# The last head group of a linear-attention numerator: six matmuls over 72 rows against four over 108

## The chip, the cores and the metric

The kernel runs on one core of one Trainium2 chip. Its metric is the device time in microseconds (us) from one launch. Times of several runs are given by their median.

TensorE (PE) multiplies matrices; its weight loads (PEld) and its matmuls are separate instructions that overlap. VectorE (DVE), ScalarE (ACT) and GpSimd (POOL) do elementwise work. SyncE (SP) issues most transfers (DMAs). ACT and POOL also issue some. Each engine takes its instructions strictly in the order of its own queue.

## The reference

The whole layer is a gated linear-attention block with a feed-forward branch, in float32, with 2048 tokens, width 576, 32 heads of 18, and a hidden width of 4608:

```
xn  = layernorm(x)
q, k, v = xn @ wqkv, split into 32 heads of 18
pq, pk  = q @ w_phi, k @ w_phi            (per head, 18 x 18)
phi_q   = concat(softmax(pq), softmax(-pq))    # 36 features per head
phi_k   = concat(softmax(pk), softmax(-pk))
kv  = phi_k^T v        (per head, 36 x 18);   z = sum over tokens of phi_k
num = phi_q kv;        den = phi_q z + 1e-6
s   = (num / den) @ wo
g   = silu( (silu(xn @ w_gate) * (xn @ w_up)) @ w_down )
out = x + s * g
```

The change concerns `num`, which the code computes in a function called `numer`.

## The kernel before

**Precision.** Matmuls run on operands of a shortened float32 type (`F32R`). To keep accuracy every operand is held as a high part and a low part: `split(hi, lo, src)` casts `src` into `hi` on ACT and subtracts on DVE to get `lo`. A product then takes three matmuls, high by high, low by high and high by low.

**Stages.** Tokens are normalised and transposed (0 to about 80 us), then for each of 16 token tiles of 128 the key features and the values are computed and `kv` is summed in three PSUM banks `kvp` (`k_tile`, `kv_step`, up to about 217 us). Then comes the setup for the queries (lines 530 to 565): the bank's column of `z` is spread into `zb`, each bank is masked so that only the 18 x 18 blocks of one head stay (`km`, line 558), and split into `KVH` and `KVL` (line 560, helper lines 62 and 63). From about 220 to 455 us runs the query stage; after about 476 us the feed-forward products run to the end.

**Head groups.** Seven heads make a group of 126 columns. There are `NG` = 5 groups: four of 126 and a last one of `NL` = 72 columns (4 heads). For each group and each of the two softmax signs (`s`), `KVH[:, 2 * g + s]` is a block-diagonal matrix of kv.

**The query stage.** `q_tile` makes the unnormalised features of 128 tokens, `e` of 128 x 1152 (first 576 columns for one sign, then 576 for the other), scales them by the softmax sums and the denominator (line 626, the last write of `e`) and returns them. `numer` takes two such tiles (`QS` = 256 tokens). For each group it transposes the group's columns of both tiles and both signs with PE into `pt` (line 638, four transposes), splits them into `ph` and `pl` (line 641), and adds up six matmuls into `po` (line 645): `KVH` by `ph`, `KVL` by `ph`, `KVH` by `pl`, each for two signs. The result is split into `oh` and `ol`. The last group goes first. Its result takes another form: the high part is written into `om` (tile name `km`) twice, and 36 rows of the low part are put under each by a transfer (`km<-lo`, line 653), so that `om` has `NK` = 108 rows and the projection with `wo` needs two matmuls for this group and not three. `project` multiplies by `wo` (line 672) and stores. There are 8 calls of `numer`.

**Order of work.** The program's order is a wish: a planner places each instruction on its engine's queue by costs that it assumes, and the marks `tc.high_priority()` and `tc.issue_after(...)` move single ones. So PE mixes three things in the query stage: the query products (line 96, `p<-QH,X` and `p<-QL,X`), the numerators and projections, and early strips of the feed-forward products (`early_tile`, line 96, `pe<-X,wh` and `pe<-X,wl`), which depend on neither. Their weights come through `raw` (line 113) and the casts of lines 66 to 68.

**SP's queue at the seam.** In order: stores of `sum_dram` (lines 366, 367), loads of `wo` (577), loads of `tl` (592), a store of `h_dram` (136), then the `raw` loads (113).

**Buffers.** Pools marked `reuse_waits="tile"` hand memory on when the old tile's readers are done. `phi` is the name of the key features' two buffers, which nothing uses after the last `kv_step`.

Of the kernel before, what the change touches and what calls it, by code (L numbers as in the profile page):

```python
# [9 lines left out]
F32 = mybir.dt.float32  # L10
F32R = mybir.dt.float32r
# [6 lines left out]
S, D, H, DH, F = 2048, 576, 32, 18, 4608  # L18
P = 128
# [7 lines left out]
GW = GH * DH  # L27
GROUPS = [(g * GW, min(GW, D - g * GW)) for g in range((D + GW - 1) // GW)]
NG = len(GROUPS)
NL = GROUPS[-1][1]  # L30
NK = NL + NL // 2
QS = 256
EARLY = 4
FIRST = (EARLY + 1, EARLY)
# [7 lines left out]
def heads(ap):  # L42
    return ap.rearrange("p (h d) -> p h d", d=DH)


def spread(ap, n):
    return ap.unsqueeze(2).to_broadcast([P, n, DH])
# [3 lines left out]
def gated_hedgehog_kernel(ctx: ExitStack, tc, x, w_qk, w_v, w_phi, wo, w_gu, w_tail, w_down, ident_in, mask_in, out):  # L51
# [5 lines left out]
    nc = tc.nc  # L57
# [3 lines left out]
    def split(hi, lo, src):  # L61
        nc.scalar.copy(hi, src)  # L62
        nc.vector.tensor_sub(lo, src, hi)  # L63
# [19 lines left out]
    def block(t):  # L83
        return t // HT, (t % HT) // 4, slice((t % 4) * P, (t % 4 + 1) * P)
# [55 lines left out]
    with ExitStack() as att:  # L140
        const = att.enter_context(tc.tile_pool(name="const", bufs=1))
        ident = const.tile([P, P], F32, name="ident")
# [15 lines left out]
        with ExitStack() as wst:  # L158
# [144 lines left out]
            kk = kst.enter_context(tc.tile_pool(name="kk", bufs=2, side="right", reuse_waits="tile"))  # L303
# [134 lines left out]
            def k_tile(t):  # L438
                i0, j0, cols = block(t)
                pk = kps.tile([P, 2, 512], F32, name="p2")  # L440
                for i in range(2):
                    w = slice(i * HALF, (i + 1) * HALF)
                    xw(pk[:, i, 0:HALF], i0, j0, cols, KVWH[:, :, :, w], KVWL[:, :, :, w], True)
                phi = kk.tile([P, 2 * D], F32, name="phi", bufs=2)
                sm = softmax_parts(pk, phi)
                nc.vector.reciprocal(sm, sm)
                nc.vector.tensor_mul(heads(phi), heads(phi), spread(sm, 2 * H))
                return phi
# [18 lines left out]
            for p in range(8):  # L467
                k = (p + 4) % 8
                ts = [k // 4 * HT + k % 4 + 4 * j for j in range(2)]
                if p < 2:  # L470
                    for j, t in enumerate(ts):
                        phi = k_tile(t)
# [56 lines left out]

        with ExitStack():  # L530
            qc = att.enter_context(tc.tile_pool(name="qc", bufs=1, reuse_waits="tile"))
            KVH = qc.tile([GW, 2 * NG, GW], F32R, name="KVH")
            KVL = qc.tile([GW, 2 * NG, GW], F32R, name="KVL")
            zb = qc.tile([P, 2 * D], F32, name="zb")
            zc = qc.tile([GW, 12], F32, name="zc")
            m4 = mask.rearrange("p h d -> p (h d)")
            banks = [(i, 4 if i < 2 else 2, GROUPS[2 * i][1]) for i in range(3)]
            for i, n, w in banks:
                nc.scalar.copy(zc[0:w, 4 * i:4 * i + n], kvp[i][0:w, 0:n, w])
            z2, oz = zb.rearrange("p (s n) -> p s n", s=2), GROUPS[-1][0]  # L540

            def z_rows(d, g, s):
                w = GROUPS[g][1]
                nc.tensor.matmul(d, zc[0:w, 2 * g + s:2 * g + s + 1].to_broadcast([w, P]), ident[0:w, 0:w],
                                 start=True, stop=True)

            for s, name in enumerate(("vx", "vy")):
                zp = kps.tile([P, 512], F32, name=name)
                for g, (o, w) in enumerate(GROUPS[:-1]):
                    z_rows(zp[:, o:o + w], g, s)  # L550
                nc.scalar.copy(z2[:, s, 0:oz], zp[:, 0:oz])
            zp = kps.tile([P, 512], F32, name="vx")
            for s in range(2):
                z_rows(zp[:, s * NL:(s + 1) * NL], NG - 1, s)
            nc.scalar.copy(z2[:, :, oz:D], zp[:, 0:2 * NL].rearrange("p (s n) -> p s n", s=2))
            for i, n, w in banks:
                km = qc.tile([GW, 4, GW], F32, name="km")
                nc.vector.tensor_mul(km[0:w, 0:n, 0:w], kvp[i][0:w, 0:n, 0:w],
                                     m4[0:w, 0:w].unsqueeze(1).to_broadcast([w, n, w]))
                split(KVH[0:w, 4 * i:4 * i + n, 0:w], KVL[0:w, 4 * i:4 * i + n, 0:w], km[0:w, 0:n, 0:w])  # L560

        raw_x(order[7], 0, 1)
        raw_x(order[7], 2, 3)
# [4 lines left out]
        with ExitStack() as qst:  # L568
            qw = qst.enter_context(tc.tile_pool(name="qw", bufs=1, reuse_waits="tile"))
            qk = qst.enter_context(tc.tile_pool(name="qk", bufs=2, reuse_waits="tile"))  # L570
# [8 lines left out]
            def split_wo():  # L579
# [4 lines left out]
                for a, t in enumerate((WOH, WOL)):  # L584
                    nc.sync.dma_start(t[NL:NK, NG - 1].bitcast(F32), WOH[a * (NK - NL):a * (NK - NL) + NK - NL, NG - 1].bitcast(F32))

# [20 lines left out]
            def q_tile(t):  # L607
                i0, j0, cols = block(t)
                pq = qps.tile([P, 2, 512], F32, name="p2")
                for i in range(2):  # L610
                    w = slice(i * HALF, (i + 1) * HALF)
                    xw(pq[:, i, 0:HALF], i0, j0, cols, QH[:, :, :, w], QL[:, :, :, w], True)
                e = qk.tile([P, 2 * D], F32, name="e", bufs=4)
                r = softmax_parts(pq, e).rearrange("p (s h) -> p s h", s=2)
                ez = qk.tile([P, 2 * D], F32, name="ez", bufs=1)
                nc.vector.tensor_mul(ez, e, zb)
                y = qk.tile([P, 2 * H], F32, name="y")
                nc.vector.reduce_sum(y, heads(ez), axis=AX.X)
                y2 = y.rearrange("p (s h) -> p s h", s=2)
                nc.vector.scalar_tensor_tensor(y2[:, 0], r[:, 0], DEN_EPS, y2[:, 0], op0=ALU.mult, op1=ALU.add)  # L620
                nc.vector.tensor_mul(y2, y2, r[:, ::-1])
                den = qk.tile([P, H], F32, name="den")
                nc.vector.tensor_add(den, y2[:, 0], y2[:, 1])
                nc.vector.reciprocal(den, den)
                nc.vector.tensor_mul(y2, r[:, ::-1], den.unsqueeze(1).to_broadcast([P, 2, H]))
                last_e.append(nc.vector.tensor_mul(heads(e), heads(e), spread(y, 2 * H)))
                return e

            def numer(es):
                oh = qk.tile([GW, NG - 1, QS], F32R, name="oh", bufs=1)  # L630
                ol = qk.tile([GW, NG - 1, QS], F32R, name="ol", bufs=1)
                om = qc.tile([NK, 2, QS], F32R, name="km")
                for g in (NG - 1, *range(NG - 1)):
                    o, w = GROUPS[g]
                    pt = qps.tile([GW, 2, QS], F32, name="pt", bufs=2)
                    for s in range(2):
                        for j, e in enumerate(es):
                            nc.tensor.transpose(pt[0:w, s, j * P:(j + 1) * P], e[:, s * D + o:s * D + o + w], ident)
                    ph = qk.tile([GW, 2, QS], F32R, name="ph", bufs=2)
                    pl = qk.tile([GW, 2, QS], F32R, name="pl", bufs=2)  # L640
                    split(ph[0:w], pl[0:w], pt[0:w])
                    po = pt[:, 0]
                    for k, (a, p) in enumerate(((KVH, ph), (KVL, ph), (KVH, pl))):
                        for s in range(2):
                            nc.tensor.matmul(po[0:w], a[0:w, 2 * g + s, 0:w], p[0:w, s], start=k + s == 0, stop=k + s == 3)
                    if g < NG - 1:
                        split(oh[0:w, g], ol[0:w, g], po[0:w])
                        continue
                    lo = qk.tile([NL, QS], F32R, name="lo", bufs=1)
                    nc.scalar.copy(om[0:NL], po[0:NL].unsqueeze(1).to_broadcast([NL, 2, QS]))  # L650
                    nc.vector.tensor_sub(lo, po[0:NL], om[0:NL, 0])
                    for a in range(2):
                        nc.sync.dma_start(om[NL:NK, a].bitcast(F32), lo[a * (NK - NL):a * (NK - NL) + NK - NL].bitcast(F32))
                return oh, ol, om

            def project(b, oh, ol, om, last):
                for j in range(QS // P):
# [3 lines left out]
                    for i in range(2):  # L661
# [7 lines left out]
                        mm = [(a[:, g, jc], bw[:, g, n]) for g in range(NG - 1) for a, bw in ((oh, WOH), (oh, WOL), (ol, WOH))]  # L669
                        mm += [(om[:, a, jc], bw[0:NK, NG - 1, n]) for a, bw in enumerate((WOH, WOL))]  # L670
                        for k, (a, bw) in enumerate(mm):
# [495 lines left out]
    for i, n, f in units:  # L1167
# [3 lines left out]
        if f >= FIRST[i]:  # L1171
            w = kept.pop() if i and kept else ready.pop(0)
# [6 lines left out]
        if n % 2 == 0:  # L1179
            g = {"f": (f, units[units.index((i, n, f)) + 1][2]), "h": [h]}  # L1180
# [58 lines left out]
```

## Time and profile before

| what | value |
|---|---|
| median of 3 runs | 1592.99 us (1592.48 to 1593.02) |
| profiled execution, its own time | 1592.74 us |
| its span, first to last instruction | 1590.6 us |
| granted TensorE clock, mean | 0.999 |
| matmuls | 9383 |
| PE, PEld busy | 1578.2 us (99%), 1416.1 us (89%) |
| DVE, ACT, POOL busy | 1166.5 (73%), 724.8 (46%), 662.3 us (42%) |

An instruction's row has its start, its duration, its engine, its line, the tiles that it writes and reads, its shape, and in square brackets the time that the engine stood idle before it with what ended the wait. "x2" is two instructions merged into one row from the first start to the last end. A busy PE is modelled: matmuls overlap in a pipeline, so the distance between two starts is what a matmul takes of PE's time, and not its duration.

### The profile page before, as it was taken

To read this page: it belongs to the slowest core of one execution; us is meant where nothing else is said; L and a number is where in the kernel's file an instruction comes from. 1 tells how busy PE (TensorE), PEld (TensorE's weight loads), DVE (VectorE), ACT (ScalarE), POOL (GpSimd) and SP (SyncE) were. 2 spreads that over 40 slices of the span, in tenths; PEclk is the share of its full clock that TensorE was granted. 3 is DMA by queue.
4 is the path that set the end of the run, shared out by engine and by line. 5 is a ranking of instruction groups with operands and counts; after the bars stand their busy time and mean duration, and the time that the engine had idled before them with its cause. 6 is when DMAs were issued, how large, how long until landed. Compare 5 with 4: busy or idle time off the path is not lost.

```text
span 1590.6 us, 25333 instructions
## 1 busy us (share of the span) xinstructions
PE 1578.2 (99%) x9383; PEld 1416.1 (89%) x9383; DVE 1166.5 (73%) x1729; ACT 724.8 (46%) x1403; POOL 662.3 (42%) x714
## 2 busy tenths in 40 slices
PE   9999999999999999999999999999999999999998
PEld 6899998999988988988888898888888888888887
DVE  7777769999946778887777778645767667666677
ACT  5633345455435654454544554454443343333334
POOL 3676762433116535554545445223324324133133
PEclk9999999999999999999999999999999999999999
DMA  9622244445447554555455453974545655555445
GB/s 306 200 82 81 95 145 129 119 122 163 165 175 245 174 178 174 176 177 180 174 174 200 163 186 116 337 219 151 154 139 156 192 177 160 176 184 184 142 118 179
DMA packets 124044, 269.03 MB, mean 169 GB/s; under 512 B 13194, under 2 KB 54858, under 8 KB 122642
## 3 DMA queue, kind: packets, MB, share of 16 engines
q1 hardware_dynamic: 108476, 245.49, 47.2%
q0 software_dynamic: 3552, 12.59, 2.7%
q10 hardware_dynamic: 11894, 9.35, 1.8%
q8 instruction: 74, 1.21, 0.3%
q14 instruction: 48, 0.39, 0.1%
HBM read 167.53 MB, written 99.09 MB: 168 GB/s over the span
## 4 chain that ended last, share of the span: by engine, by line
PE 67%; DVE 1%; POOL 1%; DMA 0%; issue 0%; ACT 0%; SPq 0%; POOLq 0%
PE px L790 25%; PE pd L911 24%; PE pw L790 12%; PE py L790 6%; DMA hb<-h_dram 0%; POOL acc L949 0%; PE pe L96 0%; DVE w L63 0%; DVE hh L63 0%; DMA out<-acc 0%; ACT w L62 0%; POOL ld L769 0%; DVE X L940 0%; POOL ha L1050 0%; DVE X L1073 0%
## 5 line engine op out<-in xcount | busy, mean ns | idle before, releaser
L911 PEld LDWEIGHTS pd<-dw,hh 128*128 128x128 f32 x3012 | 423.4, 188 | 22.4 <-ACT pd L966 1.5
L911 PE MATMUL pd<-dw,hh 128*128 128x288 f32 x3012 | 437.6, 295 | 1.9 <-ACT pd L966 0.7
L790 PE MATMUL px<-X,w 128*128 128x512 f32 x1512 | 385.7, 390 | 0.0
L790 PEld LDWEIGHTS px<-X,w 128*128 128x128 f32 x1512 | 274.6, 188 | 46.0
L790 PE MATMUL pw<-X,w 128*128 128x512 f32 x744 | 188.8, 389 | 0.0
L790 PEld LDWEIGHTS pw<-X,w 128*128 128x128 f32 x744 | 139.6, 188 | 28.9
L1073 DVE TENSOR_TENSOR acc<-pd,acc 128x576 f32<-128x576 f32 x128 | 96.2, 752 | 92.7 <-PE pd L911 92.1
L824 DVE TENSOR_TENSOR s<-pw,s 128x512 f32<-128x512 f32 x126 | 86.4, 687 | 90.3 <-ACT s L819 80.0
L819 ACT COPY s<-px 128x512 f32<-128x512 f32 x126 | 73.8, 586 | 145.4 <-PE px L790 145.3
L63 DVE TENSOR_TENSOR hh<-ha,hh 128x512 fp32r<-128x512 f32 x140 | 112.0, 826 | 19.6 <-ACT hh L62 19.3
L62 ACT CAST hh<-ha 128x512 fp32r<-128x512 f32 x140 | 82.7, 619 | 94.2 <-PE pd L911 68.7
L1045 POOL TENSOR_TENSOR hb<-hb 128x512 f32<-128x512 f32 x34 | 46.3, 1362 | 157.5 <-DVE hb L836 156.5
L96 PE MATMUL pe<-X,wh 128*128 128x512 f32 x340 | 106.0, 396 | 1.3 <-DVE h L135 0.6
L63 DVE TENSOR_TENSOR w<-ld,w 128x512 fp32r<-128x512 f32 (+1 forms) x96 | 77.2, 806 | 35.1 <-ACT w L62 34.1
L790 PE MATMUL px<-X,wt 128*128 128x512 f32 x252 | 98.0, 389 | 0.0
L790 PE MATMUL py<-X,w 128*128 128x512 f32 x378 | 96.5, 390 | 0.0
L1058 POOL TENSOR_TENSOR ha<-ha 128x512 f32<-128x512 f32 x34 | 52.6, 1563 | 102.1 <-DVE hh L63 102.1
L766 POOL TENSOR_TENSOR ts<-ld 128x256 f32<-128x256 f32 x32 | 26.8, 837 | 151.3 <-issue 72.6
L1032 POOL TENSOR_TENSOR h<-ha,hb 128x512 f32<-128x512 f32 x34 | 44.3, 1304 | 106.9 <-DVE ha L840 76.3
L62 ACT CAST w<-ld 128x512 fp32r<-128x512 f32 (+1 forms) x96 | 52.7, 550 | 74.9 <-POOL ld L769 42.3
L844 ACT COPY py<-px 128x512 f32<-128x512 f32 x63 | 36.1, 572 | 108.8 <-PE px L790 97.3
L790 PEld LDWEIGHTS py<-X,w 128*128 128x128 f32 x378 | 68.3, 188 | 10.8
(293 smaller groups left out, 3219.7 us busy)
## 6 DMA issues: line engine op xcount, KB each, us to landing
w_dram<-w SPq DMA_DIRECT2D x90, 512.0 KB
w<-w_dram SPq DMA_DIRECT2D x90, 512.0 KB
wt<-t_dram SPq DMA_DIRECT2D x62, 336.0 KB
ld<-in_B_w_gu SPq DMA_DIRECT2D x32, 512.0 KB
rt<-in_B_w_down SPq DMA_DIRECT2D x33, 288.0 KB
rb<-in_B_w_down SPq DMA_DIRECT2D x33, 288.0 KB
w_dram<-w SPq DMA_DIRECT2D x30, 256.0 KB
w<-w_dram SPq DMA_DIRECT2D x30, 256.0 KB
```

Of the source, the lines that this page charges most:

```text
L62: nc.scalar.copy(hi, src)
L63: nc.vector.tensor_sub(lo, src, hi)
L96: last = nc.tensor.matmul(ps, l, r, start=n == 0, stop=n == len(pairs) - 1)
L790: nc.tensor.matmul(ps, l, r, start=first and n == 0, stop=last and n == len(mm) - 1, skip_group_check=True)
L819: snaps.append(nc.scalar.copy(t, ps))
L824: nc.vector.tensor_add(t, ps, t)
L844: copies.append(nc.scalar.copy(yp, xp))
L911: nc.tensor.matmul(ps, l, r, start=first and n == 0 and m == 0, stop=n == len(hs) - 1 and m == 2, skip_group_check=True)
L1032: sub(s, g["h"][0][0], g["h"][0][1])
L1045: nc.gpsimd.tensor_add(a21, a21, g["h"][1][1])
L1058: sub(a12, a12, g["h"][0][0])
L1073: nc.vector.tensor_add(a2, pd[:, :, 0:HALF], a2)
```

## The change

The last group of 72 columns is divided per sign into 54 and 18 columns. The first 54 columns of both signs are stacked into 108 rows, and get three matmuls as before (`KVP[:, 0]` by high, `KVP[:, 1]` by high, `KVP[:, 0]` by low). The last 18 columns of both signs are stacked three times into 108 rows: 36 rows take the low part and 72 the high part, and against them stand `KVH`, `KVH` and `KVL` rows in `KVP[:, 2]`, so that one matmul does all three products. In the changed code:

- `q_tile` writes a second tile `et` of 128 x 2 x 108 with two copies on ACT after the last write of `e`, and `numer` transposes this group's columns from `et` (108 wide for 72).
- The split of this group has one ACT cast of 108 rows and two DVE subtractions of 256 elements for one of 512 (the second in place, over 36 rows).
- The last bank's split goes to `km2`, which lies in a `phi` buffer, and ten transfers on SP lay it out into `KVP`: four of 54 rows and six of 18 rows, with 72 numbers (288 bytes) a row.
- `KVH` and `KVL` become two matrices shorter each.
- In `numer` the last group comes second and not first.

```
+N3 = NK // 2
...
-            KVH = qc.tile([GW, 2 * NG, GW], F32R, name="KVH")
-            KVL = qc.tile([GW, 2 * NG, GW], F32R, name="KVL")
+            KVH = qc.tile([GW, 2 * NG - 2, GW], F32R, name="KVH")
+            KVL = qc.tile([GW, 2 * NG - 2, GW], F32R, name="KVL")
...
+            km2 = kk.tile([P, 2 * D], F32R, name="phi", bufs=2)[0:NL, 0:4 * NL].rearrange("p (a s n) -> p a s n", a=2, s=2)
+            km2 = [km2[:, a] for a in range(2)]
...
-                split(KVH[0:w, 4 * i:4 * i + n, 0:w], KVL[0:w, 4 * i:4 * i + n, 0:w], km[0:w, 0:n, 0:w])
+                kh, kl = (t[0:w, 4 * i:4 * i + n, 0:w] for t in (KVH, KVL)) if n == 4 else km2
+                split(kh, kl, km[0:w, 0:n, 0:w])
+            KVP = qc.tile([NK, 3, NL], F32R, name="KVP")
+            for s in range(2):
+                for a, t in enumerate(km2):
+                    nc.sync.dma_start(KVP[s * N3:(s + 1) * N3, a].bitcast(F32), t[0:N3, s].bitcast(F32))
+                for b, t in enumerate((km2[0], *km2)):
+                    r = (2 * b + s) * DH
+                    nc.sync.dma_start(KVP[r:r + DH, 2].bitcast(F32), t[N3:NL, s].bitcast(F32))
...
-                return e
+                et = qk.tile([P, 2, NK], F32, name="et", bufs=2)
+                o = GROUPS[-1][0]
+                e2 = e.rearrange("p (s n) -> p s n", s=2)
+                nc.scalar.copy(et[:, 0].rearrange("p (s n) -> p s n", s=2), e2[:, :, o:o + N3])
+                nc.scalar.copy(et[:, 1].rearrange("p (b s n) -> p b s n", b=3, s=2),
+                               e2[:, :, o + N3:D].unsqueeze(1).to_broadcast([P, 3, 2, DH]))
+                return e, et
...
-                for g in (NG - 1, *range(NG - 1)):
+                for g in (0, NG - 1, *range(1, NG - 1)):
...
-                            nc.tensor.transpose(pt[0:w, s, j * P:(j + 1) * P], e[:, s * D + o:s * D + o + w], ident)
+                            src = e[0][:, s * D + o:s * D + o + w] if g < NG - 1 else e[1][:, s]
+                            nc.tensor.transpose(pt[0:w if g < NG - 1 else NK, s, j * P:(j + 1) * P], src, ident)
...
-                    split(ph[0:w], pl[0:w], pt[0:w])
...
-                    for k, (a, p) in enumerate(((KVH, ph), (KVL, ph), (KVH, pl))):
-                        for s in range(2):
-                            nc.tensor.matmul(po[0:w], a[0:w, 2 * g + s, 0:w], p[0:w, s], start=k + s == 0, stop=k + s == 3)
+                    if g < NG - 1:
+                        split(ph[0:w], pl[0:w], pt[0:w])
+                        mm = [(a[0:w, 2 * g + s, 0:w], p[0:w, s]) for a, p in ((KVH, ph), (KVL, ph), (KVH, pl)) for s in range(2)]
+                    else:
+                        nc.scalar.copy(ph[0:NK], pt[0:NK])
+                        nc.vector.tensor_sub(pl[0:NK, 0], pt[0:NK, 0], ph[0:NK, 0])
+                        nc.vector.tensor_sub(ph[0:2 * DH, 1], pt[0:2 * DH, 1], ph[0:2 * DH, 1])
+                        mm = [(KVP[:, a], p) for a, p in ((0, ph[0:NK, 0]), (1, ph[0:NK, 0]), (0, pl[0:NK, 0]), (2, ph[0:NK, 1]))]
+                    for k, (a, p) in enumerate(mm):
+                        nc.tensor.matmul(po[0:w], a, p, start=k == 0, stop=k == len(mm) - 1)
```

## The prediction

> **What bounds the kernel now.** I read the page's shares first, then the busy time by stretches of the query stage (220 to 455 us), then the waits of PE's weight loads there, and last the single instructions around the last group.
>
> ```profile
> span 1590.6 us, 25333 instructions
> PE 1578.2 (99%) x9383; PEld 1416.1 (89%) x9383; DVE 1166.5 (73%) x1729; ACT 724.8 (46%) x1403; POOL 662.3 (42%) x714
> ```
> ```profile
> 260.00:300.00 40.00, 39.97 (x293) 37.94 (x292) 37.66 (x62) 20.05 (x38) 13.63 (x28) 1.00 0.39 111
> ...
> 440.00:460.00 20.00, 19.99 (x131) 17.46 (x130) 7.60 (x13) 7.75 (x16) 0.00 (x0) 1.00 0.13 41
> ```
> ```profile
> PEld p L672 <- ACT oh L62: 1.7, 8, 0.3
> PEld pt L645 <- DVE pl L63: 1.6, 6, 0.3
> PEld pt L638 <- DVE e L626: 0.9, 3, 0.4
> ```
>
> The columns of the stretches are length, then busy time and count of PE, PEld, DVE, ACT and POOL, then PE's clock, the DMA share and GB/s. PE is busy 39.97 of 40 us and DVE 37.66 of 40. So in the query stage PE never runs dry, because early feed-forward strips fill what DVE's softmax chain leaves free; from 440 us DVE is idle more than half the time and PE still has strips to do. The three waits (total us, times, longest) come to 4.2 us in the whole stage. Time therefore follows the sum of PE's work: what PE no longer does is gained, as long as no new wait is longer than its cover.
>
> **The matmuls removed.** Distances between starts:
>
> ```profile
> 442.00 0.40 PE L645 MATMUL pt<-ph,KVL 72*72 72x256 f32 x2
> 442.23 0.40 PE L645 MATMUL pt<-pl,KVH 72*72 72x256 f32 x2
> 442.46 0.40 PE L645 MATMUL pt<-ph,KVH 126*126 126x256 f32 x2
> ```
> ```profile
> 454.49 0.29 PE L672 MATMUL p<-WOL,oh 126*128 126x288 f32 x1
> 454.62 0.30 PE L672 MATMUL p<-WOH,ol 126*128 126x288 f32 x1
> 454.75 0.30 PE L672 MATMUL p<-WOH,km 108*128 108x288 f32 x1
> 454.89 0.29 PE L672 MATMUL p<-WOL,km 108*128 108x288 f32 x1
> ```
>
> Two matmuls of 72 rows by 256 take 0.23 us, so one takes 0.115 us. More rows cost nothing: the starts of 126-row and 108-row matmuls of 288 columns lie 0.13 and 0.14 us apart alike. Two fewer in each of 8 calls: 16 x 0.115 = 1.84 us off PE.
>
> **Wider transposes.** Four in each call, 32 in all, now load 108 columns for 72:
>
> ```profile
> L638 PEld LDWEIGHTS pt<-ident,e x160: 112/139/143, 243.7 to 448.2; 128*126 128x126 f32 x128, 128*72 128x72 f32 x32
> ```
> ```profile
> 436.85 0.38 PE L638 MATMUL pt<-ident,e 128*72 128x128 f32 x2
> 436.99 0.48 PE L96 MATMUL pe<-X,wh 128*128 128x512 f32 x1
> ```
> ```profile
> 447.92 0.63 PE L638 MATMUL pt<-ident,e 128*126 128x128 f32 x4
> 448.31 0.38 PE L672 MATMUL p<-WOL,oh 126*128 126x288 f32 x1
> ```
>
> The load takes 112 ns (the least, 72 columns) and 139 ns (the median, 126), 0.5 ns a column. The transposes' own distance grows alike: 0.14 / 2 = 0.070 us at 72 and 0.39 / 4 = 0.098 us at 126. So 36 more columns cost 0.018 us, times 32 = 0.58 us. Bounds: 0, if the strip's neighbour hides it, and the whole step to 126, 32 x 0.028 = 0.9 us.
>
> The Trainium skill, "TensorE: Matmul & The Clock Gate", section "LDWEIGHTS (loading the stationary operand)", says that a load takes as many ns as its columns divided by 1.2, whatever the rows. By it 36 columns are 30 ns, 0.96 us in all, an estimate from that page, and the sum would be 0.4 us worse. The trace agrees that rows don't count and shows 0.5 ns a column where the page has 0.83; the measurement decides.
>
> **DVE's subtraction in two.**
>
> ```profile
> L63 DVE TENSOR_TENSOR pl<-pt,ph x40: 676/682/692, 260.3 to 449.3; 126x512 fp32r<-126x512 f32 x32, 72x512 fp32r<-72x512 f32 x8
> ```
> ```profile
> L651 DVE TENSOR_TENSOR lo<-pt,km x8: 408/416/421, 262.7 to 443.3; 72x256 fp32r<-72x256 f32 x8
> ```
>
> Two of 256 are 2 x 416 = 832 ns for 682, so 0.15 us more in each call, 1.2 us of DVE. PE's strips cover it, except where PE stands waiting for `pl`: 6 of 40 groups above. For 8 groups that is 1.2 times 0.15 = 0.2 us. Without that cover it is 1.2 us; that is its upper bound, and 0 the lower one.
>
> **ACT's gathers.** Two copies after each of 16 `e`, SBUF to SBUF, 108 elements each. Nearest row:
>
> ```profile
> L62 ACT CAST w<-ld x96: 396/620/625, 462.8 to 1322.0; 128x512 fp32r<-128x512 f32 x64, 128x256 fp32r<-128x256 f32 x32
> ```
>
> From 396 ns at 256 elements to 620 at 512, 0.875 ns each: 108 elements give 0.27 us. A broken access pattern (18 at a time, read three times) may cost more; the 256-element row, 0.40 us, is my upper bound. That is 32 x 0.27 = 8.6 us of ACT (to 12.8), in a stage where ACT is busy half of the time, as above. On the path lie at most the two copies of the pair's second tile, 0.54 us from the last write of `e` to this group's transposes; group 0 now goes first and needs no gather, and its four transposes and the strips lie in between. I take 0 on PE; uncovered it is 8 x 0.54 = 4.3 us. Behind the gathers on ACT wait the casts of `ph`, which PE's products need half a microsecond later; the strips cover that too.
>
> **Order of the groups and `om`.** One cast and one DVE subtraction make the rows that the transfers take, later now by one group:
>
> ```profile
> 443.73 1.53 SPq L653 DMA_DIRECT2D km<-lo  x2
> ```
> ```profile
> 452.13 0.29 PE L672 MATMUL p<-WOH,km 108*128 108x288 f32 x1
> ```
>
> A group's products take 6 x 0.115 = 0.7 us and its casts about 1 us, against 452.13 - 445.26 = 6.9 us from the end of the issue to the first use, in the last call, the tightest one. Cost 0; if a wait for other steps ate all of it, the same transfers would hold the projection by what exceeds 6.9 us.
>
> **The ten small transfers.** They wait for DVE's last split and then stand on SP ahead of what SP does at the seam:
>
> ```profile
> 226.90 0.36 SPq L366 DMA_DIRECT2D sum_dram<-shi  x1
> 228.26 0.36 SPq L367 DMA_DIRECT2D sum_dram<-slo  x1
> 229.06 0.36 SPq L366 DMA_DIRECT2D sum_dram<-shi  x1
> 230.43 0.36 SPq L367 DMA_DIRECT2D sum_dram<-slo  x1
> ```
> ```profile
> 241.00:243.00 2.00, 2.00 (x15) 1.75 (x14) 1.90 (x5) 1.83 (x4) 1.84 (x4) 1.00 0.45 180
> 243.00:245.00 2.00, 1.91 (x16) 1.70 (x15) 2.00 (x3) 2.00 (x3) 1.83 (x3) 1.00 0.05 12
> ```
> ```profile
> 242.14 0.84 ACT L66 CAST wh<-raw 128x768 fp32r<-128x768 f32 x1
> ```
> ```profile
> 245.50 0.42 DVE L68 TENSOR_TENSOR wh<-raw,wh 32x256 fp32r<-32x256 f32 x1
> ```
> ```profile
> 253.12 0.68 DVE L135 TENSOR_TENSOR h<-pe,h 128x512 f32<-128x512 f32 x1
> ```
>
> An issue costs 0.36 us (a store, above) to 1.53 / 2 = 0.77 us (`km<-lo`, SBUF to SBUF with 36 rows). I take 0.77, the like kind: 7.7 us for ten, from about 225 to 233, where the first store stood at 226.90. The stores, the loads of `wo` and `tl`, and the `raw` loads move back by at most 6 us; some of it comes back, since SP idled between the four stores. The burst of transfers that ends near 242 would end near 246, and so the cast at 242.14 and DVE's step that ends at 245.92 move 4 us, to 250. PE needs these weights when the strip before them is done, which the product at 253.12 closes: 3 us are left. Behind the delayed cast on ACT wait the casts of `wo`, needed only by the first projection, and DVE's chain may slip 1 to 2 us, which the strips fill. Cost 0 on PE, bounds 0 and about 4 us. The transfers' own landing, near 235, is far from the first use in the first call, past 260 (the first `pl` is at 260.3 in the row above).
>
> No cost, one line each: the last bank's split has the same shape as before; its buffer `phi` is free after the last `kv_step`; shorter `KVH` and `KVL` move the later tiles by some hundred bytes, whose waits I can't see from here and put at plus or minus 1 us.
>
> **The sum.** The profiled execution took 1592.74 us, 0.25 below the median, for a span of 1590.6. Off 1.84, on 0.58 and 0.2: 1.06 us less, 1591.7 us there and 1591.9 us against the median. That is less than 0.2% of 1592.99 (3.2 us), about what a measurement of this kernel can tell from no change, which puts the lines at 1589.8 and 1596.2.
>
> **Rivals.**
> 1. *Gathers on the path, slower.* If the planner puts the last group's transposes right behind group 0's and PE has no strip there, each call waits for two gathers and the extra subtraction: 8 x (0.54 + 0.15) = 5.5 us, less 1.26: 1597.2 us. For it: PE already waited three times for `e` (0.9 us). Against: those waits were 0.3 us each, and the group moved behind another. It decides from 4.5 us of waits, 0.55 a call.
> 2. *SP's queue, slower.* If an issue takes 1.5 us or the burst is pushed by over 7 us, the next strip's weights come late by what exceeds 7 us. At 15 us for the ten, PE loses some 5 us: 1596.9 us. Against: no SBUF transfer here took over 0.77 us.
> 3. *Waits go as well, faster.* The new order gives PE group 0's transposes straight from `e`. If two of the three waits of 4.2 us went (2.5), the time would be 1589.4 us. Against: they belong to all five groups, and one group is touched.
> 4. *PE isn't the bound, no gain.* Freed slots are filled by nothing and the time stays at 1593.0. The Trainium skill, "Perfetto Trace Analysis", section "Identifying the Most-Contended Engine", holds matmul busy time a poor measure and the loads' busy share the better one; the page of this profile has 89% there. The start distances speak against it here: one matmul follows another at 0.115 us with 72-column and 126-column loads alike, so the stream sets the pace.
>
> **Chances.** Forecast 0.62, rival 4 0.15, rival 1 0.08, rival 2 0.04, rival 3 0.11. Faster is rival 3 (0.11), slower rivals 1 and 2 (0.12), within 0.2% the forecast and rival 4 (0.77). The bounds around the forecast: best 1593.0 - 1.84 = 1591.2, with 1 us for moved tiles 1590.2; worst with 0.9, 1.2 and a part of SP's 4 us, 1595.3. To hold 8 in 10 the range reaches into rival 3 and stops short of rivals 1 and 2: 1589.3 to 1595.3 us.
>
> **What would show it.** PE with 9367 matmuls and the four at 0.115 us; transposes 108 wide with loads near 130 ns; ACT's gathers near 0.27 us; DVE with 8 more subtractions; SP with ten issues near 0.77 us from 225 us, the first `sum_dram` store after 230, and the `wh<-raw` cast near 246 with no new wait of PE. Wrong would be: a wait of line 638 for ACT in most calls, a gap in the strips near 250 us, or feed-forward weights that start later than the query stage ends earlier.

## The result and the profile after

| | before | after |
|---|---|---|
| median | 1593.0 us (4 runs, 1592.5 to 1593.3) | 1602.6 us (4 runs, 1600.8 to 1604.6) |
| ratio | | 1.0064 [1.0052, 1.0076] |
| profiled execution, span | 1592.74 us, 1590.6 us | 1600.83 us, 1599.0 us |

The changed kernel is 9.6 us slower; 1591.9 us were predicted, at most 1595.3. Two of its four executions were granted a mean clock of 1.000 (1600.83 and 1601.18 us) and two 0.998 (1604.10 and 1604.64 us), and the profile shows the fastest. That the clock makes these 3.3 us is not shown: among the ten executions of a_late, below, those with 0.998 took 1593.81 to 1595.63 us and the others 1593.16 to 1595.54.

The page of the changed kernel:

```profile
span 1599.0 us, 25377 instructions
PE 1577.4 (99%) x9367; PEld 1414.4 (88%) x9367; DVE 1170.3 (73%) x1737; ACT 733.6 (46%) x1437; POOL 662.3 (41%) x714
```

PE has the 16 matmuls less and is busy 0.8 us less, in a span that is 8.4 us longer. Busy time by stretches (length, then PE, PEld, DVE, ACT, POOL with counts, PE's clock, DMA share, GB/s) of the kernel before:

```profile
245.00:250.00 5.00, 5.00 (x26) 4.28 (x25) 4.96 (x6) 2.60 (x5) 0.00 (x0) 1.00 0.52 161
480.00:520.00 40.00, 39.76 (x196) 33.82 (x195) 27.12 (x40) 22.59 (x44) 23.37 (x24) 1.00 0.65 226
```

and of the changed kernel:

```profile
241.00:243.00 2.00, 1.08 (x8) 1.11 (x9) 1.93 (x5) 1.97 (x3) 0.00 (x0) 1.00 1.00 292
...
245.00:250.00 5.00, 2.92 (x17) 2.40 (x16) 3.26 (x4) 2.98 (x5) 3.75 (x8) 1.00 0.40 156
260.00:300.00 40.00, 40.00 (x283) 37.35 (x282) 37.02 (x59) 22.39 (x43) 13.60 (x28) 1.00 0.43 128
440.00:460.00 20.00, 20.00 (x126) 17.21 (x125) 16.42 (x28) 10.70 (x22) 0.00 (x0) 1.00 0.14 48
480.00:520.00 40.00, 36.06 (x168) 29.27 (x168) 29.29 (x38) 19.92 (x41) 27.00 (x28) 1.00 0.83 289
```

From 260 to 300 us PE is as full as before. PE stands idle at two places where it was full: at the seam (241 to 250 us) and at the opening of the feed-forward (480 to 520 us). A third part of the loss, 3 us, is spread in small waits over the stage between them (the table further on). And from 440 to 460 us DVE is busy 16.4 us where it was 7.6: the query stage's chain is not over yet.

**The seam.** SP, ACT and PE of the changed kernel:

```profile
225.04 1.72 SPq L568 DMA_DIRECT2D KVP<-phi  x2
226.80 2.20 SPq L571 DMA_DIRECT2D KVP<-phi  x3
229.04 1.44 SPq L568 DMA_DIRECT2D KVP<-phi  x2
230.52 2.18 SPq L571 DMA_DIRECT2D KVP<-phi  x3
232.81 0.41 SPq L367 DMA_DIRECT2D sum_dram<-shi  x1
...
239.37 0.43 SPq L137 DMA_DIRECT2D h_dram<-h  x1
240.25 1.36 SPq L114 DMA_DIRECT2D raw<-in_B_w_gu  x2
```
```profile
240.22 0.68 ACT L320 ACTIVATE e<-e 128x576 f32<-128x576 f32 x1 [7.52 <-DVE e L317]
...
242.21 0.60 ACT L132 ACTIVATE h<-pe 128x512 f32<-128x512 f32 x1
...
244.12 0.69 ACT L320 ACTIVATE e<-e 128x576 f32<-128x576 f32 x1
247.02 0.83 ACT L67 CAST wh<-raw 128x768 fp32r<-128x768 f32 x1 [2.21 <-DMA raw<-in_B_w_gu]
247.76 0.28 ACT L641 COPY et<-e 128x108 f32<-128x108 f32 x1
```
```profile
241.92 0.37 PE L97 MATMUL p<-QH,X 128*128 128x288 f32 x1 [1.73 <-DVE e L317]
...
248.09 0.32 PE L656 MATMUL pt<-ident,et 128*108 128x128 f32 x1 [2.08 <-ACT et L641]
```

Read it from the transfers on. Ten issues of 0.72 to 0.86 us end at 232.7, the first store of `sum_dram` stands at 232.81 (226.90 before), the `raw` loads at 240.25 (234.68). The cast `wh<-raw` on ACT waits for them until 247.02. Behind it on ACT stand the two gathers of `et`, though their `e` has been done since 243.7, and on PE the transposes that read `et`, with the strips behind them: 2.08 us. The other wait, 1.73 us, is for DVE to empty the bank of the query products. The strip's `Silu` (242.21) now stands between the two exps, with a load of ACT's function table before it and one behind it (240.92 and 242.83, 1.28 us each); in the kernel before it stood ahead of both. On DVE a sum of the first tile stands ahead of the second tile's first reduction. That the planner orders so because the store of `h_dram`, which hands on the `Silu`'s buffer, comes late (239.37 for 234.14) is likely and not shown.

**The opening.** SP's first loads of feed-forward weights, before and after:

```profile
457.89 1.30 SPq L738 DMA_DIRECT2D ld<-in_B_w_gu  x2
```
```profile
470.48 1.30 SPq L762 DMA_DIRECT2D ld<-in_B_w_gu  x2
```

They wait for memory that the last projection frees (457.4 us before, 470.0 after). What PE has left of strips then is the cover under which they are loaded, combined and split: the first `px` product came at 476.03 us, 18.1 us after the load; now at 479.74 us, 9.3 us after. The changed kernel's ACT and PE then show what is late:

```profile
513.86 0.41 ACT L63 CAST w<-ld 128x256 fp32r<-128x256 f32 x1 [3.71 <-POOL ld L793]
```
```profile
516.88 1.42 PE L814 MATMUL px<-X,w 128*128 128x512 f32 x5 [2.48 <-ACT s L843]
```

ACT stands at a cast of weights that POOL has not combined, and the copy `s` that would free a bank for PE is queued behind it.

To compare all runs I use PE's lost time: for each matmul, the distance to the next one's start less the median distance of its kind in the kernel before, summed by stretch (us), beside the end of the last projection:

```
                                   217-262  262-460  480-520  last projection
before                                 0.8      5.8      0.5    457.4
after                                  4.6      8.8      5.4    470.0
before + transfers  (b_kvp)            5.1      4.6      2.7    467.4
before + gathers    (b_gather)         1.0     13.1      6.8    473.7
 same, group second (b_gather2)        1.0      8.1      0.2    459.9
before, group second (b_order)         1.1      6.3      0.2    458.2
matmuls alone       (a_four)           1.3      7.6      3.5    463.9
after, no gathers   (a_nog)            4.3      6.3      5.4    467.9
after, late transfers (a_late)         1.2      7.0      3.2    463.3
 same, no gathers   (a_late_nog)       1.2      7.6      3.8    463.1
 same, strips held  (a_late_g4)        1.1     12.4      0.2    462.6
before, tails on GpSimd (before_tl)    1.0      9.1      0.2    460.2
matmuls, tails on GpSimd (a_four_tl)   1.1     13.0      0.3    462.0
```

Each row is one execution. Those of a_nog (1599.42 us, median 1595.42) and a_late_g4 (1598.60, median 1595.54) are the longest of their kernels and show more than their medians have.

### The profile page after: what moved, and what is told of

The parts are those of the page before. It is cut to its first block, busy times and chain, and to the rows that moved or that the text cites. A ratio compares the mean times of both kernels' runs of the same rounds, so it can differ in the third digit from the quotient of the medians.

```text
span 1599.0 us, 25377 instructions
## 1 busy us (share of the span) xinstructions
PE 1577.4 (99%) x9367; PEld 1414.4 (88%) x9367; DVE 1170.3 (73%) x1737; ACT 733.6 (46%) x1437; POOL 662.3 (41%) x714
## 4 chain that ended last, share of the span: by engine, by line
PE 90%; DMA 3%; DVE 3%; POOL 1%; ACT 1%; issue 1%; SPq 1%; ACTq 0%; POOLq 0%
PE px L814 24%; PE pd L935 24%; PE pw L814 12%; PE p L97 7%; PE py L814 6%; PE pe L97 4%; PE p L696 4%; PE kvp L333 2%; PE pt L669 2%; PE vx L421 1%; PE pt L656 1%; DMA raw<-in_B_w_gu 1%; PE vw L421 1%; PE vx L97 1%; PE vy L97 1%
```

## The experiments

Each ratio is to the kernel before, run beside the changed one each time; its median there was 1592.0 to 1592.7 us, against 1593.0 above, so the ratios compare better than the microseconds. The letters Q and G in the expectations stand for two theories, SP's queue and the gathers.

**Transfers alone** (b_kvp). The kernel before with the last weights in a tile `KVT` and the ten transfers into an unused `KVP`:

```
+            KVP = qc.tile([NK, 3, NL], F32R, name="KVP")
+            for s in range(2):
+                for a, t in enumerate(km2):
+                    nc.sync.dma_start(KVP[s * N3:(s + 1) * N3, a].bitcast(F32), t[0:N3, s].bitcast(F32))
...
```

> The kernel before with the ten small transfers added on SP, into a KVP that nothing reads (its last-group weights stand in a tile of their own). Theory Q (SP's queue: the transfers push the stores and the raw loads at the seam, the cast of raw on ACT comes late and everything behind it): PE loses 2 to 4 us between 235 and 250 us, 1595 to 1597 us. Theory G (the gathers on ACT are what costs, at the seam and over the whole query stage): first sum_dram store still moves to about 232 us, but the time stays within 1 us of 1593.

1596.55 us, 1.0023 [1.0013, 1.0033], as Q has it. Its waits at the seam (the second is at 262.33 us, for the second tile's `e`):

```profile
PE p L96 <- DVE e L316: 1.7, 1, 1.7
PE pt L649 <- DVE e L637: 1.4, 1, 1.4
PE pe L96 <- DVE h L135: 0.9, 1, 0.9
```

The 1.7 us are there without any gather. The same wait stands in every kernel that has the transfers at this place and in none of the others.

**Gathers alone** (b_gather), with the last group first as before:

```
-                return e
+                et = qk.tile([P, 2, 104], F32, name="et", bufs=2)
+                for s in range(2):
+                    nc.scalar.copy(et[:, s], e[:, (s + 1) * D - 104:(s + 1) * D])
+                return e, et
```

> The kernel before with two ACT copies of 104 columns after each e, and the last group's transposes reading from them; six matmuls, old order, no transfers. Theory G: the softmax chain slips by about 8 us (last projection near 465 us for 457.5), PE waits for the copies and the feed-forward opening loses its cover: 1596 to 1599 us. Theory Q: within 1 us of 1593.

1612.04 us, 1.0116 [1.0101, 1.0131], far over both theories. The same with the group second (b_gather2):

```
-                for g in (NG - 1, *range(NG - 1)):
+                for g in (0, NG - 1, *range(1, NG - 1)):
```

> The kernel before with two copies of 104 columns per tile on ScalarE (as in the run of 1612 us) but the last group second in the order instead of first; 78 strip matmuls are left behind the last projection (41 in the run of 1612 us, 77 in the kernel before). If the gathers cost only because the last group's transposes came first and because the cover went, the time is that of the kernel before: 1592.0 to 1593.5 us. If ScalarE's queue is the cost whatever the order (its copies stand behind the exps), PE's waits for the gathered columns stay at several us and the time is 1600 us or more.

1594.81 us, 1.0018 [1.0009, 1.0027], between the two cases of the expectation. PE's waits for the gathers between 262 and 470 us, first and second in order:

```profile
PE pt L644 <- ACT et L631: 6.5, 3, 3.8
```
```profile
PE pt L644 <- ACT et L631: 1.0, 1, 1.0
```

The order is worth 16 to 17 us to the gathers. By itself it is worth nothing (b_order, the same two lines in the kernel before):

> The kernel before with the last group second and not first, nothing else. If the new order of groups has a part in the loss, over 1595 us with the last projection later than 460 us. Both theories on the transfers and on the gathers say it has none: 1592 to 1594 us.

1592.89 us, 1.0007 [0.9998, 1.0017].

**The transfers on GpSimd's queue** (a_poolq), the changed kernel with `nc.sync.dma_start` of the ten made `nc.gpsimd.dma_start`:

> The changed kernel with the ten transfers issued by GpSimd and not by SP. Theory Q: the first sum_dram store is back near 227 us, the raw cast near 242, no wait of 2 us for the gather at 248, and the feed-forward opening keeps its cover: about 1593 to 1595 us. Theory G: only the 2.2 us wait at the seam goes, the rest stays: 1598 to 1600 us.

1603.15 us, 1.0065 [1.005, 1.008]: nothing is won. Ten issues of some 0.5 us stand ahead of POOL's sums, the stores of `sum_dram` are late again, and PE's wait for the bank is longer:

```profile
PE p L97 <- DVE e L317: 3.7, 1, 3.7
```

**The gathers on DVE** (a_dve): the last scaling of `e` split in three, two of them writing `et`:

```
+                nc.vector.tensor_mul(e4[:, :, 0:hm], e4[:, :, 0:hm], y2[:, :, 0:hm].unsqueeze(3).to_broadcast([P, 2, hm, DH]))
+                nc.vector.tensor_mul(et[:, 0].rearrange("p (s h d) -> p s h d", s=2, d=DH), e4[:, :, hm:H - 1], ...)
+                last_e.append(nc.vector.tensor_mul(et[:, 1].rearrange("p (b s d) -> p b s d", b=3, s=2), ...))
...
```

> The changed kernel with no gathers on ACT: DVE's last scaling of e is divided in three, and two of the parts write the gathered columns at once. Theory G: last projection back to about 460 us, feed-forward opening without its 4 us, 1594 to 1597 us. Theory Q: the seam still costs 2 to 4 us and its slip stays: 1598 us or more.

1598.69 us, 1.0032 [1.0018, 1.0047], some 4 to 5 us less than the changed kernel: the seam still costs, as Q has it, but the gathers no longer stand behind the cast.

**The transfers late** (a_late). The changed kernel; the last split and the ten transfers move into `lay_out()`, called after `split_wo()`:

```
+            def lay_out():
+                km2 = qk.tile([P, 7, P], F32R, name="th", bufs=1).rearrange("p a n -> p (a n)")
...
+                with tc.issue_after(exps[-1].ins):
+                    split(km2[:, 0], km2[:, 1], kv_last)
...
```

> The changed kernel with the ten transfers on SP behind the raw loads (the last bank is split and laid out after the second query tile); gathers on ACT as in the change. Theory Q+G (both cost, by delays in in-order queues): the 1.9 us gap near 239 and the late cast go, the second tile's e is done near 259 us again, but the waits for the gathers stay in the stage: 1597 to 1606 us. If the transfers were all of it: 1592 us.

1594.10 us, 1.0016 [1.0006, 1.0025], under what Q and G together allowed and over what the transfers alone did. By the ratios this gives back three quarters of the loss (0.48 of 0.64 per cent). SP's queue has its old order again, and the transfers stand between the `raw` loads:

```profile
226.82 0.36 SPq L367 DMA_DIRECT2D sum_dram<-shi  x1
...
248.92 0.73 SPq L598 DMA_DIRECT2D KVP<-th  x1
249.71 1.44 SPq L601 DMA_DIRECT2D KVP<-th  x2
...
255.08 0.33 SPq L114 DMA_DIRECT2D raw<-in_B_w_gu  x1
```

With the transfers late, nothing is won with the gathers on DVE (a_late_dve)

> The same with the gathers written by DVE's scaling and none on ACT. Theory Q+G: neither the seam nor the gathers cost, the last projection ends near 457 to 460 us, the feed-forward opening keeps its cover, and the saved matmuls show: 1591 to 1594 us. If something else in the change costs (wider rows, split subtraction, other buffers), it stays over 1597 us.

1595.49 us, 1.0024 [1.0014, 1.0034]; on GpSimd it is slower (a_late_pool)

> The same with the gathers on GpSimd. If it is ACT's queue that the gathers hurt, 1591 to 1595 us, like the one with DVE. If it is the added step between e and the transposes, wherever it runs, PE waits for et as with ACT: 1597 us or more.

1597.71 us, 1.0041 [1.0026, 1.0056], where single copies of 0.28 us took up to 1.00 us and PE waited 1.8 us for them; and nothing is won with the last group third (a_late_3rd, `(0, 1, NG - 1, *range(2, NG - 1))`)

> The late lay-out with the last group third in place of second, so that some 2 us more of PE's work lie between the end of a tile's e and the transposes that read the gathered columns. Taking the group from first to second was worth 17 us to the gathers alone (1612.0 to 1594.8). If their wait is still what is left, 1592.0 to 1593.0 us; if the rest lies elsewhere, 1594.1 us as with the group second, or more, since the sums and the projections behind the last group start later.

1594.85 us, 1.0016 [1.0007, 1.0026].

**Without gathers.** The transposes of the last group read 108 contiguous columns of `e`, with the transfers late (a_late_nog) and early (a_nog):

```
-                et = qk.tile([P, 2, NK], F32, name="et", bufs=2)
...
-                return e, et
+                return e, e.rearrange("p (s n) -> p s n", s=2)[:, :, D - NK:D]
```

> The late lay-out (1594.1 us) without the gathers (other data in the last group, as above), with its ten transfers. If the gathers are what is left of the loss (two copies per tile alone cost 2.6 us in the old form with the group second), 1591.5 us (1590.8 to 1592.3), under the kernel before. If the late transfers or the matmuls hold it, 1593.5 to 1594.5 us.

1594.75 us, 1.0017 [1.0007, 1.0027]: what is left with the transfers late is not the gathers.

> The changed kernel (1602.6 us) without the gathers, its ten transfers early on SP's queue. If transfers and gathers add (3.5 us for the transfers alone beside the kernel before, 2.6 for the gathers), 1595.5 us (1594 to 1597); the other 5 to 7 us of the loss then come only from both together: the gathers stand on ScalarE behind the cast that the late raw load holds up, and PE's transposes behind them. If the transfers at that place cost the 8.5 us that moving them gave back whatever the gathers, 1600 us.

1595.42 us, 1.0024 [1.0014, 1.0035]. So the four cases are: neither early transfers nor gathers 1594.75, gathers alone 1594.10, early transfers alone 1595.42, both 1602.64 us. The costs don't add: some 7 us (6.5 by the ratios) come only from both together. The runs without gathers lie between 1594.65 and 1599.42 us and don't touch those of the changed kernel. The seam of a_nog has the bank's wait; the wait for `et` at 248.09 is gone, and later, at 263.49, PE waits for the second tile's `e`:

```profile
PE p L97 <- DVE e L317: 1.7, 1, 1.7
PE pt L650 <- DVE e L637: 1.4, 1, 1.4
```

So the times show that the two edits meet, and the traces only part of how: the changed kernel's waits for `et` are 2.08 and 0.9 us, and where the rest of the 7 us lies can't be read from a profile of a_nog that is only 1.6 us shorter.

**The matmuls alone** (a_four): neither gathers nor transfers, `KVP` read from a part of `KVH`:

```
-            KVP = qc.tile([NK, 3, NL], F32R, name="KVP")
+            KVP = KVH[0:NK, 0:3, 0:NL]
...
-                    lay_out()
```

> Of the change only the four wider matmuls, the split subtraction and the order are left: no gathers (the last group's transposes read 108 contiguous columns of e) and no small transfers (the weights are read from a part of KVH), so the last group's values are other data. If the sum of the prediction was right for PE's side, 1591.0 to 1592.2 us against 1592.2 of the kernel before. If the four-matmul form is itself what makes the query stage run behind (43 strip matmuls are left behind the last projection, as in the changed kernel, 77 before), 1594 us, as the late lay-out measured.

1596.32 us without one execution of 4047.09 us, 1.0022 [1.0011, 1.0032]. Here is what the prediction's sum was about, with nothing around it, and it is slower too. The seam is clean. The last projection ends 6.5 us later, the weights' load follows it,

```profile
464.41 1.31 SPq L749 DMA_DIRECT2D ld<-in_B_w_gu  x2
```

the first `px` product comes at 473.89 us, only 9.5 us behind that load, and the opening loses 3 us more than before:

```profile
510.50 1.65 PE L801 MATMUL px<-X,w 128*128 128x512 f32 x6 [2.53 <-ACT s L830]
```

Up to there PE was nearly as full as before (1.8 us more lost from 262 to 460 us). It had spent its strips sooner: 45 of their matmuls were left at 457.4 us, where the kernel before has 74.

**Holding the strips back.** The last strips of unit 3 may start only behind the last projection's first copy (a_late_g4), behind the projection before (a_late_g5, `outs[-5]`), and the first of these in the changed kernel (after_g4):

```
+                with tc.issue_after(outs[-4].ins) if (f, i) == (EARLY - 1, 0) else ExitStack():
+                    early_tile(f, i, ...)
```

> The late lay-out (1594.1 us) with one more thing: both halves of the early strip of unit 3, first row block, may start only behind the first copy of the last projection. 84 strip matmuls stand behind the last projection in PE's order instead of 44 (77 in the kernel before). Theory that the opening of the feed-forward is short of cover: PE's excess of 480 to 520 us goes from 3.2 to about 0.5 us and the time to 1591.4 us (1590.5 to 1592.3), under the kernel before by 1 us. Rival, that the strips were filling waits of the query stage's chain: the same 3 us come up as gaps in 430 to 475 us, and the time stays at 1594 us or goes above it.

1595.54 us, 1.0018 [1.0008, 1.0028].

> The same as the late lay-out with the held strips, but held only behind the last copy of the projection before the last: 69 strip matmuls are left behind the last projection. If cover is what counts, and 10 us of it (44 matmuls) cost 3 us while 18.7 us (77) cost none, 69 matmuls (15.6 us) give a time between the two: 1591.5 to 1592.5 us. If the strips were needed earlier, 1594 us or more.

1595.42 us, 1.0021 [1.0011, 1.003].

> The changed kernel (1602.6 us) with the same two half strips held behind the first copy of the last projection: 84 strip matmuls behind it instead of 43. The cover theory: the opening's excess of 5.4 us shrinks to 0.5 to 1.5 us, the seam at 235 to 262 us keeps its 4.4 us, and the time is 1597 us (1595.5 to 1599). The rival (strips needed where they stood): 1602 us or more.

1607.11 us, 1.0092 [1.0077, 1.0107]. In a_late_g4 the opening's loss goes (0.2 us), as my theory said, and comes back between 440 and 460 us, where the chain now runs with nothing beside it (part of it is a halved clock, shown at the end); it ends hardly sooner than in a_late (462.6 against 463.3 us). The theory that cover at the opening is all that is missing falls: the strips covered waits in both places.

**Room on DVE.** I thought that DVE, busy over 90% of the query stage, made the chain late with its extra subtraction, and moved the tails' eight subtractions to GpSimd, in a_four (a_four_tl) and as a control in the kernel before (before_tl):

```
-                nc.vector.tensor_sub(t, t, hi)
+                nc.gpsimd.tensor_sub(t, t, hi)
```

> The four wider matmuls alone (1596.5 us, other data in the last group and no gathers or transfers, as before) with one more edit: the eight subtractions of the tails (128x896, 1.08 us each on VectorE) go to GpSimd, 8.7 us less for VectorE in the query stage. 72 strip matmuls are left behind the last projection instead of 43. Theory that VectorE, busy 36 to 39 of each 40 us there, sets the pace of the query stage and that the four-matmul form lost by adding to it: the last projection ends near 458 us instead of 464, the 2.7 us wait at 507 us goes, and the time is 1591 to 1592.5 us. Rival, that the products or the order of the group hold it: the chain still ends near 464 us and the time stays above 1594.5 us.

1597.44 us, 1.0034 [1.0023, 1.0044].

> The control: the kernel before with the same edit of the tails' subtractions. It has its cover already (78 strip matmuls behind the last projection, 77 without the edit), and its PE has almost no gaps to close: 1592.2 us, within 1 us, if cover is what the edit buys. If room on VectorE is worth time by itself, 1591 us or less. Were GpSimd's longer subtractions late for the tails' stores, 1593 us or more.

1595.38 us, 1.0019 [1.001, 1.0029]. The theory failed in both. There were 72 and 78 strip matmuls left and the opening was full, and still the kernel before lost 3 us: PE's lost time in the query stage rose from 5.8 to 9.1 us, in small waits. But the edit is no neutral control. The subtraction takes 2.1 us on GpSimd for 1.08 on DVE, and DVE's instructions beside it are longer:

```profile
262.01 2.11 POOL L600 TENSOR_TENSOR tl<-tl,th 128x896 f32<-128x896 f32 x1 [17.31 <-ACT th L599]
263.22 2.11 DVE L616 TENSOR_TENSOR ez<-e,zb 128x1152 f32<-128x1152 f32 x1
265.99 0.50 PE L645 MATMUL pt<-ph,KVH 126*126 126x256 f32 x2 [0.42 <-DVE pl L63]
```

The product `ez` took 1.35 us each time in the kernel before; here it took 2.11 and once 2.31 us beside such a subtraction. In all, DVE's instructions that overlap the eight of them are 3.8 us longer than their medians before. That some of PE's new waits come from this is likely (the one above is for the DVE instruction right behind `ez`); how much of the 3 us is not shown.

## Why the prediction was wrong

- **Sizes.** All but one were right. 9367 matmuls, and the four some 0.12 us apart; loads of 108 columns at 132 ns (130 predicted); the split subtraction 0.416 + 0.406 us for the 0.832 predicted; gathers of 0.28 us (0.27); ten issues of 0.72 to 0.86 us (0.77); first store at 232.81 (after 230). The 0.58 us for wider transposes were misread: from one transpose to the next the traces have a median of 109 ns with 72 and with 126 columns before and with 108 after, and some 28 ns where other work follows. The 0.070 and 0.098 us were a group of two and one of four, not narrow and wide. Without the term the sum would have been faster still, so it is not why the prediction failed. The changed kernel's forms:

```profile
L656 PEld LDWEIGHTS pt<-ident,et x32: 128/132/134, 248.1 to 452.8; 128*108 128x108 f32 x32
```
```profile
L665 DVE TENSOR_TENSOR pl<-pt,ph x8: 414/416/425, 264.3 to 454.7; 108x256 fp32r<-108x256 f32 x8
```
```profile
L666 DVE TENSOR_TENSOR ph<-pt,ph x8: 403/406/406, 264.6 to 455.0; 36x256 fp32r<-36x256 f32 x8
```
```profile
L641 ACT COPY et<-e x16: 263/282/293, 247.8 to 452.2; 128x108 f32<-128x108 f32 x16
```

- **"Cost 0 on PE" of the ten transfers: the first step that failed.** The raw cast came at 247.02 where 246 was foreseen, so the delay was right, and the cover given for it ("3 us are left", up to the strip at 253.12) was of the wrong work. I counted only who needs the weights. What is queued behind the cast on ACT was named as the casts of `wo`; the change's own gathers stand there too, and PE's transposes behind them. The other wait, for the query products' bank, comes with another order on ACT and DVE in every kernel with the early transfers; I treated the order around them as fixed. Alone the transfers cost 0.23 per cent, 3.7 us, in b_kvp: inside the bounds of 0 and 4 us given for them, and not the 0 in the sum.
- **"I take 0" for the gathers.** Right for themselves once the transfers are late: 1594.10 us with them, 1594.75 without. Wrong in company: the bound of 4.3 us assumed that a gather costs its own duration, and in a queue in order it costs the wait of whatever stands ahead. Rival 1 had the place (transposes that wait for ACT); that its price of 5.5 us is near what the pair cost (7) is luck, for it counted short waits in each call, and in the profile there was one of 2.08 us at the seam and one of 0.9 us later. Rival 2, with 4 in 100, had SP's queue, but by issues of 1.5 us, and they took 0.72 to 0.86; PE waited no more than 0.2 us for the strips' weights.
- **"Time therefore follows the sum of PE's work": the deepest error.** With all of PE's saving and none of the rest, a_four lost 3.5 us by its ratio, where the sum promised a gain of about 1. PE is full in the query stage because strips fill it; the time at which the stage's chain ends is another quantity, and that sets when the feed-forward's weights may be loaded. The prediction read DVE's idle time after 440 us as room. It is the tail of a chain whose end is a due date: 18.1 us, filled with strips, lie between the load and the first product that needs it; in a_four 9.5. Holding strips back showed that this cover is not all: it took the loss from the opening and put one into the stage.
- **Rival 4** (freed slots are filled by nothing) had its chance on the wrong reading: the slots were filled, by strips that were needed later. The Trainium skill, "Perfetto Trace Analysis", section "Identifying the Most-Contended Engine", on which its sentence leaned, takes the loads' busy share for the better measure; here that share went from 89% to 88% in a slower kernel, and neither share told.

What is not settled: why the planner spends strips sooner in these builds, and why the gathers with the group second (2.9 us by the ratio), the matmuls alone (3.5) and, perhaps for the reason given above, the tails on GpSimd (3.0) each cost about 3 us, while the groups' order alone costs nothing that can be measured. The cover at the opening was tried and isn't all; DVE's load was tried with an edit that slows DVE in another way, and so stays open. The traces narrow it down. In a_four the chain does not fall behind a little in each call. The last scaling of the eighth tile's `e` ends at 336.3 us (337.6 before), that of the tenth at 367.6 (362.0). In between DVE splits two pieces of strip weights (341.28 and 354.17) ahead of the ninth tile's scaling (356.44), where in the kernel before the first of them stands behind it (352.39, after 350.12). b_kvp, with its six matmuls and no gathers, also has such a split ahead of that scaling (345.46) and falls back at the same place, from 2.9 us behind to 8.8. So the step belongs to an order of the queues that the four matmuls are not needed for; what brings that order about is not shown. No version tried beats the kernel before.

## What to carry to other kernels

A transfer or copy put into a queue costs what stands behind it, and two edits that are each nearly free can meet: here early transfers delayed a load, its cast held up ACT, and the new copies behind that cast held up PE, 7 us for a pair that, in the four-matmul form, cost about nothing apart (b_kvp and b_gather2 show about 3 us for either in the old form). A full PE says that filler is there, not that PE's sum is the time: ask at which time the stage's chain ends, what starts only then, and how much filler is kept for it. And where a planner orders the instructions, compare an edit with a control, and read the control's trace as well: eight subtractions moved to another engine cost 3 us here and made DVE's instructions beside them longer, while a new order of the groups cost nothing that could be measured.

## What the runs showed of the hardware that I had not expected

A stall of PE can cost more than its length. In a_late_g4 PE is idle for most of 441 to 445 us, in two waits of 1.54 and 1.07 us with 0.9 us of work between them, and then the granted clock is halved for 5 us with PE fully busy:

```profile
441.00:443.00 2.00, 0.46 (x5) 0.23 (x3) 1.84 (x3) 0.46 (x2) 0.00 (x0) 1.00 0.28 97
443.00:445.00 2.00, 0.93 (x7) 0.68 (x7) 0.83 (x2) 1.48 (x4) 0.00 (x0) 0.80 0.10 31
445.00:450.00 5.00, 5.00 (x23) 4.97 (x24) 1.42 (x5) 1.54 (x3) 0.00 (x0) 0.50 0.02 4
```

The waits of 1.73 and 2.08 us in the changed kernel's profile kept the clock at 1.00. The Trainium skill, "TensorE: Matmul & The Clock Gate", section "What's actually happening", says that the clock drops to half after an idle window of some 3.4 us that runs freely, and rises after a busy one; the trace agrees with the half, and here no single wait was as long as that: PE was busy for 1.39 of the 4 us before. No run here shows the window itself.

A small transfer from SBUF to SBUF costs SP no less issue time with 18 rows than with 54: 2.20 / 3 = 0.73 us, and 1.44 / 2 = 0.72 or 1.72 / 2 = 0.86 us, twice a store's 0.36 us. On GpSimd's queue the issues of 18 rows take 1.51 / 3 = 0.50 us:

```profile
225.48 1.51 POOL L571 DMA_DIRECT2D KVP<-phi  x3
```
